# A planner's model of transfers, groups of first scores and due times of weights changed in a fused attention and two-MLP kernel

## The chip, the cores and the metric

One core of a Trainium2 chip runs the whole program. The metric is the device time of one execution in microseconds (us); lower is better. Instructions are spread by hand over five engines: PE (matrix products; PEld are its weight loads), DVE and ACT (elementwise work), POOL (unused here) and SP, which issues the DMA transfers.

## The reference, cut to what matters

Attention over two batches of 3008 tokens, without softmax, feeds two MLPs of 2048 hidden columns. All is float32.

```python
scores = (1.0 / S) * np.matmul(z, z.transpose(0, 2, 1))   # z: (2, 3008, 64)
attn = np.maximum(scores, 0.0) ** 2
x = (u * np.matmul(attn, v)).reshape(B * S, D)            # u, v: (2, 3008, 256)
h = x @ w_in;  x = (h - np.tanh(h)) @ w_out               # w_in: (256, 2048), w_out: (2048, 256)
h = x @ w2_in; return (np.maximum(h, 0) + alpha * np.minimum(h, 0)) @ w2_out
```

## The kernel before, in words

Every float32 operand is split into a high and a low part (a cast, here `high`, and a subtraction, here `low`), and PE multiplies high by high, high by low and low by high. So one score tile or one product needs elementwise work ahead of it, and it is that work which can be late.

The 6016 tokens form 12 blocks of up to 512 (six for each batch; the sixth has 448). For a block and a tile k of 128 keys, `score` puts z z^T into a PSUM bank. There are eight banks, and two of them collect the block's result. `relu` and `square` on ACT or DVE empty a score bank, `high` and `low` split the tile, and `back` multiplies it with v and adds to the block's two result banks. A score tile that belongs to two blocks is computed once. DVE transposes it (`transpose`), SP sends it to DRAM in four parts (`flip`), and it is read back for the other block (`load` of `l`). Scores are made in groups: `GROUPS` says how many tiles a group has, `LEADS` how many products ahead of its first use it stands on PE.

The MLPs' weights come as float64 words; `split_f64` makes high and low parts of them: one 512 KB load, six DVE instructions (L468 to L490) and one on ACT (L470) for each of 32 pieces. Pieces of the second MLP go back to DRAM (`spill`) until they are wanted. `W2_DUE` and `W1_DUE` spread the pieces' due times over a stretch of the attention part. From about 440 us on PE works on the MLPs (`front`, L658, and `back`, L726).

The order on every engine is set when the program is written: class `Plan` lists all operations, gives each a due time from PE's own order, and plays an event loop with assumed durations (`run`). Each engine takes, among the operations that are ready and have room, the one with the earliest due time; the order that results is what the chip executes, in that order on each engine. In this loop a transfer of 256 KB has `op.size` = 256 x 1.024 = 262, and the lines below add 262 / 290e3 = 0.0009 us for it to `pipe`: in effect every transfer is done 0.44 us (its issue) and 4.0 us (`LANDING`) after it is taken, whatever is in flight. `RESERVE`, `READY`, `FETCH`, `CAST_PENALTY`, `OTHER_PENALTY` and `TURNED` say how early an operation may take room or which engine it prefers. None of these numbers runs on the chip; they only decide the order.

On the chip, an instruction at the head of an engine's queue that waits holds up all that stand behind it, SP's transfers included.

```python
if e == SP:
    pipe = max(pipe, busy[e]) + op.size / 290e3
    op.done = pipe + (1.95 if t < 5.0 else LANDING)
```

## Time and profile before

| what | value |
|---|---|
| time, median of 3 runs (lowest to highest) | 1502.07 us (1500.44 to 1504.58) |
| profiled execution: own time | 1504.22 us |
| profiled execution: span from first to last instruction | 1502.4 us |
| PE busy | 1485.7 us, 99% of the span |
| PE weight loads busy | 1234.7 us, 82% |
| DVE busy | 1225.2 us, 82% |
| ACT busy | 1190.9 us, 79% |
| bytes moved by DMA | 133.59 MB |
| mean granted clock of PE | 0.996 |

PE is busy nearly all the time, so the span can be shortened, with the same products, only where PE stands idle or where its clock is granted at the lower of its two levels (1.2 instead of 2.4 GHz, shown as 0.5). The page's slices show that nearly all traffic of DMA lies in the first third of the span, where DVE is at its busiest too.

### The profile page before, as it was taken

To read this page: it belongs to the slowest core of one execution; us is meant where nothing else is said; L and a number is where in the kernel's file an instruction comes from. 1 tells how busy PE (TensorE), PEld (TensorE's weight loads), DVE (VectorE), ACT (ScalarE), POOL (GpSimd) and SP (SyncE) were. 2 spreads that over 40 slices of the span, in tenths; PEclk is the share of its full clock that TensorE was granted. 3 is DMA by queue.
4 is the path that set the end of the run, shared out by engine and by line. 5 is a ranking of instruction groups with operands and counts; after the bars stand their busy time and mean duration, and the time that the engine had idled before them with its cause. 6 is when DMAs were issued, how large, how long until landed. Compare 5 with 4: busy or idle time off the path is not lost.

```text
span 1502.4 us, 19557 instructions
## 1 busy us (share of the span) xinstructions
PE 1485.7 (99%) x6823; PEld 1234.7 (82%) x6823; DVE 1225.2 (82%) x2089; ACT 1190.9 (79%) x2282; POOL 0.2 (0%) x4
## 2 busy tenths in 40 slices
PE   8999999999999999999999999999999999999998
PEld 6777787777888888888888888888888888888888
DVE  8999978999989887777777877778777877778775
ACT  8777636887668888888888888888888888888853
POOL 0000000000000000000000000000000000000000
PEclk9999999999999999999999999999999999999999
DMA  5889884788862231100000000000000000000000
GB/s 186 236 274 296 274 285 139 231 267 249 259 208 83 76 117 50 49 1 1 29 1 27 1 29 1 10 19 1 27 1 28 1 28 1 1 27 1 15 1 27
DMA packets 116898, 133.59 MB, mean 89 GB/s; under 512 B 19904, under 2 KB 78912, under 8 KB 116800
## 3 DMA queue, kind: packets, MB, share of 16 engines
q1 hardware_dynamic: 116656, 132.24, 28.0%
q8 instruction: 53, 0.87, 0.2%
q14 instruction: 45, 0.37, 0.1%
q10 hardware_dynamic: 144, 0.11, 0.0%
HBM read 77.28 MB, written 50.86 MB: 85 GB/s over the span
## 4 chain that ended last, share of the span: by engine, by line
PE 89%; DVE 4%; DMA 3%; ACT 2%; issue 1%; SPq 1%; ACTq 0%; DVEq 0%
PE bank L726 52%; PE bank L658 34%; PE bank L569 3%; DMA mm<-flip 2%; DVE mm L393 1%; DMA raw<-in_v 1%; DVE flip L611 1%; DVE mm L638 1%; ACT raw L587 1%; ACT raw L595 1%; ACT mm L366 1%; DMA raw<-in_zT 0%; DVE mm L490 0%; DVE raw L474 0%; DVE raw L476 0%
## 5 line engine op out<-in xcount | busy, mean ns | idle before, releaser
L726 PE MATMUL bank<-mm,mm 128*128 128x512 f32 (+1 forms) x4008 | 966.0, 387 | 6.6 <-DVE mm L364 5.9
L726 PEld LDWEIGHTS bank<-mm,mm 128*128 128x128 f32 x4008 | 753.6, 189 | 156.1 <-DVE mm L364 6.8
L658 PE MATMUL bank<-mm,mm 128*128 128x512 f32 (+1 forms) x2304 | 575.7, 385 | 0.0
L658 PEld LDWEIGHTS bank<-mm,mm 128*128 128x128 f32 x2304 | 432.5, 188 | 80.8
L393 DVE TENSOR_TENSOR mm<-raw,mm 128x512 fp32r<-128x512 f32 (+1 forms) x586 | 389.7, 675 | 12.8 <-ACT mm L366 7.7
L676 ACT ACTIVATE raw<-raw 128x512 f32<-128x512 f32 (+1 forms) x576 | 360.0, 626 | 3.8
L676 ACT ACTIVATE raw<-bank 128x512 f32<-128x512 f32 (+1 forms) x384 | 207.0, 587 | 114.9 <-PE bank L658 114.5
L366 ACT CAST mm<-raw 128x512 fp32r<-128x512 f32 (+1 forms) x436 | 264.4, 624 | 20.5 <-DMA raw<-in_zT 8.9
L687 DVE TENSOR_TENSOR raw<-bank,raw 128x512 f32<-128x512 f32 (+1 forms) x192 | 130.4, 679 | 162.7 <-ACT raw L676 162.6
L695 ACT ACTIVATE raw<-bank 128x512 f32<-128x512 f32 (+1 forms) x384 | 218.2, 586 | 50.1 <-PE bank L658 44.7
L685 DVE TENSOR_TENSOR raw<-bank,raw 128x512 f32<-128x512 f32 (+1 forms) x192 | 130.2, 678 | 36.3 <-ACT raw L676 28.9
L697 DVE SCALAR_TENSOR_TENSOR raw<-raw,nalpha,raw 128x512 f32<-128x512 f32 (+1 forms) x192 | 140.6, 732 | 18.9 <-ACT raw L695 18.9
L689 DVE COPY_PREDICATED raw<-raw,raw 128x512 f32<-128x512 int32 (+1 forms) x192 | 142.5, 742 | 1.2
L587 ACT ACTIVATE raw<-bank 128x512 f32<-128x512 f32 (+1 forms) x146 | 74.6, 623 | 40.4 <-PE bank L569 40.2
L595 ACT ACTIVATE raw<-raw 128x512 f32<-128x512 f32 (+1 forms) x162 | 98.6, 677 | 0.0
L366 ACT CAST mm<-mm 128x512 fp32r<-128x512 f32 (+1 forms) x90 | 55.1, 623 | 45.5 <-DMA mm<-flip 45.3
L638 DVE TENSOR_TENSOR mm<-mm,mm 128x512 fp32r<-128x512 f32 (+1 forms) x120 | 78.7, 661 | 9.3 <-ACT mm L366 8.9
L611 DVE STREAM_TRANSPOSE flip<-raw 128x512 f32<-128x512 f32 x120 | 77.1, 684 | 2.9 <-DMA mm<-flip 2.4
L364 DVE CAST mm<-raw 128x512 fp32r<-128x512 f32 (+1 forms) x156 | 63.8, 415 | 9.6 <-ACT raw L595 4.9
L569 PE MATMUL bank<-mm,mm 64*128 64x512 f32 (+1 forms) x464 | 65.1, 406 | 3.8 <-DVE raw L589 3.7
L569 PEld LDWEIGHTS bank<-mm,mm 64*128 64x128 f32 x464 | 44.2, 187 | 19.1 <-issue 5.6
L470 ACT ACTIVATE raw<-raw 128x512 int32<-128x512 int32 x32 | 20.8, 651 | 25.9 <-DVE raw L468 25.8
(33 smaller groups left out, 245.0 us busy)
## 6 DMA issues: line engine op xcount, KB each, us to landing
flip<-flip SPq DMA_DIRECT2D x100, 256.0 KB, 4.3
mm<-flip SPq DMA_DIRECT2D x80, 256.0 KB, 4.8
mm<-flip SPq DMA_DIRECT2D x40, 224.0 KB, 4.2
st<-in_moe_w_in SPq DMA_DIRECT2D x16, 512.0 KB, 5.6
st<-in_moe_w_out SPq DMA_DIRECT2D x16, 512.0 KB, 5.0
raw<-in_v SPq DMA_DIRECT2D x24, 256.0 KB, 5.1
raw<-in_uT SPq DMA_DIRECT2D x20, 256.0 KB, 5.0
xd<-raw SPq DMA_DIRECT2D x20, 256.0 KB, 3.3
```

Source lines behind the costliest of these rows:

```text
L366: nc.scalar.copy(out=out, in_=in_)
L393: lambda e: nc.vector.tensor_sub(out=r32(l)[:, :n], in0=ap(), in1=f32(h)[:, :n]), [src, h], [l])
L569: nc.tensor.matmul(out=bank(keys[half])[:, :n], lhsT=key_weights(blocks[i][0], k, low, half), rhs=query_columns(x, half, n), start=j < 2, ...
L595: nc.scalar.activation(out=ap, in_=ap, func=AF.Square)
L658: nc.tensor.matmul(out=bank(ps)[:, :n], lhsT=r32(w)[:, o:o + P], rhs=r32(x)[:, :n], start=j == 0, stop=j == len(todo) - 1)
L676: add((name, out), {ACT: us}, lambda e: nc.scalar.activation(out=f32(out)[:, :n], in_=bank(inp)[:, :n] if inp is ps else f32(inp)[:, :n], ...
L685: add(("subtract", t), {DVE: dve_us(n)}, lambda e: nc.vector.tensor_sub(out=f32(t)[:, :n], in0=src(), in1=f32(t)[:, :n]), [ps], [t], limit ...
L687: add(("series", g), {DVE: dve_us(n)}, lambda e: nc.vector.tensor_mul(out=f32(g)[:, :n], in0=src(), in1=f32(g)[:, :n]), [ps], [g], limit=b ...
L689: add(("choose", t), {DVE: 0.05 + dve_us(n)}, lambda e: nc.vector.copy_predicated(out=f32(t)[:, :n], mask=f32(mask)[:, :n].bitcast(I32), d ...
L695: add(("relu2", out), {ACT: act_psum_us(n)}, lambda e, out=out, how=how: nc.scalar.activation(out=f32(out)[:, :n], in_=src(), func=AF.Relu ...
L697: add(("leak", r), {DVE: 0.06 + dve_us(n)}, lambda e: nc.vector.scalar_tensor_tensor(out=f32(r)[:, :n], in0=f32(q)[:, :n], scalar=nalpha_s ...
L726: nc.tensor.matmul(out=bank(accs[d])[:, :n], lhsT=r32(w)[:, c0:c0 + P], rhs=r32(x)[:, :n], start=first and e == 0, stop=last and e == len( ...
```

## The change

The planner's account of transfers changes: each transfer has a size in us of its own (0.7 by default for 256 KB, 2.3 for a float64 weight piece), starts no earlier than 1.9 us after its issue and behind the one before it, lands 3.0 us after its end, and no more than eight may be in flight. The first 24 score tiles come in groups of 4, 4, 8, 8 at fixed places (`FIRST`), batch 1's first block in 12, 12, and groups stand five products ahead instead of three. The due times of the weights move: the second MLP's from 70 to 270 us into 80 to 225 us, the first MLP's from 255 to 435 us into 290 to 437 us. The last block's second half is copied by DVE for SP's queue and by ACT for ACT's queue, where it was the other way round. What is computed, and how many products, stays as it was.

```diff
-GROUPS = ((8, 8, 8), (10, 10), (8, 8), (12,), (12,))
-LEADS = 3
-FIRST = 0
-RESERVE = ((15.0, 32), (5.0, 10), (1.5, 5), (0.0, 2))
-READY, FETCH = 20.0, 16.0
-CAST_PENALTY, OTHER_PENALTY = 4.0, 16.0
-TURNED = 22.0
-MARGIN, LANDING = 1.03, 4.0
-W2_DUE, W1_DUE = (70.0, 270.0), (255.0, 435.0)
+GROUPS = (((4, 4, 8, 8), (12, 12)), ((10, 10),) * 2, ((8, 8),) * 2, ((12,),) * 2, ((12,),) * 2)
+LEADS = 5
+FIRST = (0, 0, 1, 8)
+RESERVE = ((25.0, 30), (10.0, 14), (3.0, 6), (0.0, 2))
+READY, FETCH = 20.0, 22.0
+CAST_PENALTY, OTHER_PENALTY = 6.0, 10.0
+TURNED = 18.0
+MARGIN, LANDING, FIXED, FLYING = 1.03, 3.0, 1.9, 8
+W2_DUE, W1_DUE = (80.0, 225.0), (290.0, 437.0)
...
-            op.due = end - self.fastest(op) - op.tail - (3.0 if SP in op.engines else 0.0)
+            op.due = end - self.fastest(op) - op.tail - (op.size + FIXED + 2.0 if SP in op.engines else 0.0)
...
-                pipe = max(pipe, busy[e]) + op.size / 290e3
-                op.done = pipe + (1.95 if t < 5.0 else LANDING)
+                pipe = max(t + FIXED, pipe) + op.size
+                op.done = pipe + (0.1 if t < 5.0 else LANDING)
+                flying.append(op.done)
...
+                if e == SP:
+                    flying[:] = [at for at in flying if at > t + 1e-9]
+                    if len(flying) >= FLYING:
+                        continue
...
-            cuts = ((0, n), (0, n // 2, n))[d]
-            for e, (c0, c1) in enumerate(zip(cuts, cuts[1:])):
-                engine, queue = ((ACT, nc.sync), (DVE, nc.scalar))[e]
+            for e, (engine, c0, c1) in enumerate((((ACT, 0, n),), ((DVE, 0, n // 2), (ACT, n // 2, n)))[d]):
...
+                t = FIRST[g] if b == e == 0 else when[(0, *group[0])] - LEADS
+                bursts.setdefault(t, []).append(group)
```

What this does to the order is seen at three places. The first is ACT at the start of the program, behind its table load; `in_v` tiles are raw_142 and up before, and z tiles raw_145 and raw_146. Before:

```order
L366 CAST mm_68<-raw_142 128x512
L366 CAST mm_70<-raw_143 128x512
L366 CAST mm_71<-raw_144 128x512
L366 CAST mm_73<-raw_145 128x512
L366 CAST mm_75<-raw_146 128x512
L366 CAST mm_77<-raw_147 128x512
L587 ACTIVATE raw_155<-bank_171 128x512
```

In the change the same place reads as follows (raw_140, raw_143 and raw_144 are z, raw_142 and raw_145 are v):

```order
L372 CAST mm_67<-raw_140 128x512
L372 CAST mm_69<-raw_142 128x512
L372 CAST mm_71<-raw_143 128x512
L372 CAST mm_73<-raw_144 128x512
L593 ACTIVATE raw_153<-bank_171 128x512
L372 CAST mm_74<-raw_145 128x512
L601 ACTIVATE raw_153<-raw_153 128x512
L593 ACTIVATE raw_158<-bank_173 128x512
```

Six casts stood ahead of the first relu (L587); now there are four, one of them of a tile that is loaded second. Three v tiles come after it.

The second place is SP's queue where the z tiles of batch 1 are loaded (`in_zT`, `in_z_last`), shortly before that batch's first scores. Before (L494 and L484 are spills, which wait for DVE to finish a weight piece):

```order
L743 DMA raw_152<-in_uT 128x448
L513 DMA st_163<-in_moe_w_in 128x1024
L494 DMA w_wil_0_3_243<-mm_138 128x512
L408 DMA raw_156<-in_zT 128x512
L408 DMA raw_162<-in_zT 128x512
L408 DMA raw_161<-in_zT 128x512
L484 DMA w_wih_1_3_244<-raw_149 128x512
L428 DMA raw_154<-in_z_last 128x256
```

In the change (L641 reads a flipped tile back; the last spill of the second MLP's weights is now L500):

```order
L414 DMA raw_157<-in_zT 128x512
L490 DMA w_woh_7_250<-raw_144 128x512
L500 DMA w_wol_7_251<-mm_132 128x512
L749 DMA raw_156<-in_uT 128x448
L749 DMA raw_152<-in_uT 128x448
L641 DMA mm_86<-flip_4_5_204 128x448
L641 DMA mm_69<-flip_4_5_204 128x448
L641 DMA mm_83<-flip_4_5_204 128x448
L641 DMA mm_95<-flip_4_5_204 128x448
L414 DMA raw_146<-in_zT 128x512
L414 DMA raw_153<-in_zT 128x512
L434 DMA raw_141<-in_z_last 128x256
```

The third z tile moved ahead of the weights' spills, and no spill stands between the last loads any more; all spills of the second MLP's weights are now ahead of them.

The third place is DVE where it first takes a relu (L589, then L595) of batch 1. Before, steps of weight pieces (L468, L476, L488, L490) and v splits (L393) stand just ahead of it and between:

```order
L488 TENSOR_SCALAR raw_146<-raw_149 128x512
L393 TENSOR_TENSOR mm_123<-raw_160,mm_70 128x512
L468 TENSOR_SCALAR raw_145<-st_163 128x512
L490 SCALAR_TENSOR_TENSOR mm_98<-raw_158,raw_146 128x512
L393 TENSOR_TENSOR mm_77<-raw_151,mm_118 128x512
L393 TENSOR_TENSOR mm_131<-raw_141,mm_74 128x512
L476 SCALAR_TENSOR_TENSOR raw_145<-st_163,raw_145 128x512
L393 TENSOR_TENSOR mm_122<-raw_161,mm_115 128x512
L589 TENSOR_SCALAR raw_143<-bank_172 128x512
L468 TENSOR_SCALAR raw_142<-st_164 128x512
L589 TENSOR_SCALAR raw_144<-bank_171 128x512
```

In the change:

```order
L644 TENSOR_TENSOR mm_69<-mm_69,mm_106 128x448
L644 TENSOR_TENSOR mm_83<-mm_83,mm_123 128x448
L644 TENSOR_TENSOR mm_95<-mm_95,mm_74 128x448
L399 TENSOR_TENSOR mm_68<-raw_146,mm_105 128x512
L399 TENSOR_TENSOR mm_79<-raw_153,mm_129 128x512
L595 TENSOR_SCALAR raw_145<-bank_177 128x512
L595 TENSOR_SCALAR raw_143<-bank_172 128x512
L595 TENSOR_SCALAR raw_154<-bank_176 128x512
L595 TENSOR_SCALAR raw_162<-bank_170 128x512
L595 TENSOR_SCALAR raw_144<-bank_171 128x512
```

The weights' steps are gone from here; what is left ahead of the relus are splits of flipped tiles (L644) and of z (L399).

## Rows read from the trace of the kernel before

**Rows 1.** Windows of the whole span: busy us (instructions) by engine, granted clock, DMA:

```profile
core 0: us, PE busy (x) PEld busy (x) DVE busy (x) ACT busy (x) POOL busy (x), PEclk, DMA share, GB/s
...
8.19:12.43 4.24, 0.01 (x3) 0.00 (x1) 3.42 (x7) 4.12 (x9) 0.00 (x0) 1.00 1.05 399
12.43:15.88 3.45, 3.45 (x8) 2.65 (x9) 3.45 (x7) 3.45 (x8) 0.00 (x0) 0.51 0.66 251
15.88:237.94 222.06, 219.56 (x1075) 177.45 (x1074) 200.27 (x370) 149.13 (x288) 0.00 (x0) 1.00 0.81 254
237.94:241.65 3.71, 0.00 (x1) 0.00 (x1) 3.71 (x8) 3.67 (x9) 0.00 (x0) 0.93 0.21 79
241.65:247.99 6.34, 6.34 (x19) 5.08 (x20) 5.22 (x11) 5.70 (x13) 0.00 (x0) 0.50 0.11 41
...
1498.40:1502.40 4.00, 0.00 (x0) 0.00 (x0) 0.39 (x1) 0.34 (x1) 0.00 (x0) 0.79 0.32 115
sum 1502.40, PE 1485.73 PEld 1234.68 DVE 1225.16 ACT 1190.93 POOL 0.20; mean PE 185.72 PEld 154.33 DVE 153.14 ACT 148.87 POOL 0.03
```

**Rows 2.** Waits of PE, whole span: us in total, times, longest us:

```profile
PE bank L726 <- DVE mm L364: 5.9, 2, 4.2
PE bank L569 <- DVE raw L589: 4.5, 2, 3.7
...
PE bank L726 <- DVE mm L638: 0.7, 1, 0.7
```

**Rows 3.** Timeline of PE, 8 to 36 us: start, us, what (merged):

```profile
12.43 8.73 PE L726 MATMUL bank<-mm,mm 128*128 128x512 f32 x30 [4.23 <-DVE mm L364]
21.08 3.12 PE L569 MATMUL bank<-mm,mm 64*128 64x512 f32 x24
24.14 11.20 PE L726 MATMUL bank<-mm,mm 128*128 128x512 f32 x48
```

**Rows 4.** Timeline of ACT, 4 to 15 us:

```profile
6.50 3.91 ACT L366 CAST mm<-raw 128x512 fp32r<-128x512 f32 x6 [4.28 <-DMA raw<-in_v]
10.32 1.08 ACT L587 ACTIVATE raw<-bank 128x512 f32<-128x512 f32 x2
11.28 0.63 ACT L595 ACTIVATE raw<-raw 128x512 f32<-128x512 f32 x1
```

**Rows 5.** Timeline of DVE, 3 to 15 us:

```profile
7.15 3.98 DVE L393 TENSOR_TENSOR mm<-raw,mm 128x512 fp32r<-128x512 f32 x6 [1.47 <-ACT mm L366]
11.95 0.43 DVE L364 CAST mm<-raw 128x512 fp32r<-128x512 f32 x1 [0.81 <-ACT raw L595]
```

**Rows 6.** The chain that ended last, 224 to 243 us: start, us, what:

```profile
228.44 0.69 DVE mm L490
...
229.15 0.33 SPq L494
...
230.04 5.30 DMA raw<-in_zT
...
240.99 0.61 DVE raw L589
```

**Rows 7.** DMA issues at 215.07 and at 215.62 us: KB, us to landing:

```profile
st<-in_moe_w_in SPq DMA_DIRECT2D x1, 512.0 KB, 7.3
mm<-flip SPq DMA_DIRECT2D x1, 224.0 KB, 7.6
```

**Rows 8.** Waits of all engines, 100 to 118.5 us:

```profile
ACT mm L366 <- DMA mm<-flip: 5.4, 2, 4.8
DVE raw L476 <- ACT raw L470: 3.8, 1, 3.8
```

**Rows 9.** Timeline of all engines, 1497 to 1503 us:

```profile
1498.35 1.70 SPq L775 DMA_DIRECT2D outT<-raw  x2
1498.40 0.39 DVE L364 COPY raw<-bank 128x224 f32<-128x224 f32 x1 [4.45 <-PE bank L726]
...
1499.35 0.34 ACT L366 COPY raw<-bank 128x224 f32<-128x224 f32 x1 [1.02 <-DVE raw L364]
```

**Rows 10.** DMA issues of the whole span, results: KB, median us to landing:

```profile
outT<-raw SPq DMA_DIRECT2D x3, 224.0 KB, 1.9
```

**Rows 11.** Lines by form, 16 to 440 us: count, busy us, mean ns, idle before:

```profile
L476 DVE SCALAR_TENSOR_TENSOR raw<-st,raw 128x512 uint32<-128x512 uint32 x32 | 21.8, 681 | 5.3 <-ACT raw L470 5.3
...
L468 DVE TENSOR_SCALAR raw<-st 128x512 uint32<-128x512 uint32 x32 | 13.3, 416 | 1.6 <-DMA st<-in_moe_w_in 1.6
```

More of the change, by code (lines that the diff above doesn't have):

```diff
@@ L160, in run @@
         pipe = 0.0
+        flying = []
         left = len(self.ops)
@@ L366, in copy_on, with dma @@
             nc.scalar.copy(out=out, in_=in_)
-    def dma(name, emit, reads=(), writes=(), kb=256, limit=None, horizon=1e9, holds=()):
+    def dma(name, emit, reads=(), writes=(), us=0.7, limit=None, horizon=1e9, holds=()):
         return add(name, {SP: 0.44}, lambda e: emit(nc.sync), reads, writes, limit=limit, horizon=horizon,
-                   tail=0.0, size=kb * 1.024, holds=holds)
+                   tail=0.0, size=us, holds=holds)
     def cast_us(n):
@@ L427, in need_z @@
         st2, kl = ("ks", b, c), ("kk", b, c)
-        dma(("load", st2), lambda q: q.dma_start(out=f32(st2)[:, :m], in_=z_last[b]), [], [st2], kb=128, horizon=40.0)
+        dma(("load", st2), lambda q: q.dma_start(out=f32(st2)[:, :m], in_=z_last[b]), [], [st2], us=0.35, horizon=40.0)
         add(("high", kl), cast_us(m), lambda e: copy_on(e, r32(kl)[:, :m], f32(st2)[:, :m]), [st2], [kl])
@@ L465, in u32 @@
             return f32(key).bitcast(U32)
-        dma(("load", st), lambda q: load(q, f32(st).bitcast(U32)), [], [st], kb=512, horizon=30.0)
+        dma(("load", st), lambda q: load(q, f32(st).bitcast(U32)), [], [st], us=2.3, horizon=30.0)
         add(("fields", t1), {DVE: 0.345}, lambda e: nc.vector.tensor_scalar(
@@ L529, in need_x @@
         dma(("load", st), lambda q: q.dma_start(out=stage()[:, :, :n], in_=x_dram[i][:, :, :n]),
-            [("xd", i, d) for d in range(KD)], [st], kb=512, horizon=14.0)
+            [("xd", i, d) for d in range(KD)], [st], us=1.9, horizon=14.0)
         for d in range(KD):
@@ L573, in score_group @@
             us = 3 * pe_us(max(blocks[i][2] for i, _ in pair)) * 1.02
-            us += 0.215 * ((p == 0) + (p == len(pairs) - 1))
+            us += 0.215 * ((p == 0 and lead) + (p == len(pairs) - 1))
             ops.append(add(("score", pair[0]), {PE: us}, emit, set(reads), keys, tail=0.21))
@@ L625, in score_tile @@
                     out=to.rearrange("(f r) c -> r f c", r=Q)[:, :, c + e * nt * Q:c + (e + 1) * nt * Q],
-                    in_=f32(buf)[p0:p0 + Q].rearrange("p (f c) -> p f c", c=P)[:, :, :nt * Q]), made_t, [fd], holds=[buf])
+                    in_=f32(buf)[p0:p0 + Q].rearrange("p (f c) -> p f c", c=P)[:, :, :nt * Q]), made_t, [fd], us=1.0, holds=[buf])
     flips = {}
@@ L635, in need_flipped @@
         dma(("load", l), lambda s: s.dma_start(out=f32(l)[:, :n], in_=flips[b, kb, q][e * P:(e + 1) * P]), reads, [l],
-            horizon=FETCH)
+            us=0.8, horizon=FETCH)
         add(("high", h), cast_us(n), lambda e: copy_on(e, r32(h)[:, :n], f32(l)[:, :n]), [l], [h])
@@ L743, in evacuate @@
                 dma(("load", x), lambda q, x=x, d=d: q.dma_start(out=f32(x)[:, :n], in_=uT[d * P:(d + 1) * P, t0:t0 + n]),
-                    [], [x], horizon=25.0)
+                    [], [x], us=0.85, horizon=25.0)
                 def gate(e, x=x, acc=acc):
@@ L768, in evacuate, with out @@
                 continue
-            cuts = ((0, n), (0, n // 2, n))[d]
-            for e, (c0, c1) in enumerate(zip(cuts, cuts[1:])):
-                engine, queue = ((ACT, nc.sync), (DVE, nc.scalar))[e]
+            for e, (engine, c0, c1) in enumerate((((ACT, 0, n),), ((DVE, 0, n // 2), (ACT, n // 2, n)))[d]):
                 yk = y + (e,)
+                def out(queue, yk=yk, rows=rows, c0=c0, c1=c1):
+                    queue.dma_start(out=outT[rows, b * S + s + c0:b * S + s + c1], in_=f32(yk)[:, :c1 - c0])
                 add(("copy", yk), {engine: act_psum_us(c1 - c0)}, lambda e, yk=yk, acc=acc, c0=c0, c1=c1: copy_on(
                     e, f32(yk)[:, :c1 - c0], bank(acc)[:, c0:c1]), [acc], [yk])
-                dma(("out", yk), lambda q, yk=yk, rows=rows, c0=c0, c1=c1, queue=queue: queue.dma_start(
-                    out=outT[rows, b * S + s + c0:b * S + s + c1], in_=f32(yk)[:, :c1 - c0]),
-                    [yk], [("const", "out", i, d, e)])
+                if e:
+                    add(("out", yk), {ACT: 0.4}, lambda e, out=out: out(nc.scalar), [yk], [("const", "out", i, d, e)],
+                        tail=2.0)
+                else:
+                    dma(("out", yk), out, [yk], [("const", "out", i, d, e)])
     streams = [[(0, i, k) for i in range(NBLK) for k in tiles_of[i % QB]]]
@@ L793, in attention_two_mlps_kernel @@
     for b in range(B):
-        for e, sizes in enumerate(GROUPS):
+        for e, both in enumerate(GROUPS):
+            sizes = both[b]
             qs = [e] if e < len(GROUPS) - 1 else range(e, QB)
@@ L797, in attention_two_mlps_kernel @@
             assert sum(sizes) == len(todo)
-            for size in sizes:
+            for g, size in enumerate(sizes):
                 group, todo = todo[:size], todo[size:]
-                bursts.setdefault(max(0, when[(0, *group[0])] - LEADS), []).append(group)
+                t = FIRST[g] if b == e == 0 else when[(0, *group[0])] - LEADS
+                bursts.setdefault(t, []).append(group)
     def warm(e):
@@ L821, in build @@
                 for group in bursts.get(t, ()):
-                    score_group(group, LEADS)
+                    score_group(group, t > 0)
             if 0 <= t + LOOKAHEAD < len(steps) and steps[t + LOOKAHEAD][0]:
```

2 lines of the change are left out of this document (1 added, 1 removed).

## The prediction

> **What bounds the kernel now.** I read the windows first. In the sum over the span PE is busy 1485.73 of 1502.40 us [rows 1]. The change alters no product, so all there is to win is the 16.7 us in which PE stands idle, and what its clock loses. The windows place both. PE idles 4.24 us at the start (8.19 to 12.43), and the granted clock is then 0.51 for 3.45 us; it idles 3.71 us from 237.94 on, and the clock is then 0.50 for 6.34 us; it idles 4.00 us after the last product [rows 1]. At 0.5 PE does half the work, so these slow stretches cost 3.45 x 0.49 = 1.7 us and 6.34 / 2 = 3.2 us. The list of PE's waits names the releasers: DVE casts (L364), 5.9 us in two waits of 4.2 and so 1.7 us; DVE relus (L589), 4.5 us in two waits of 3.7 and 0.8 us; a DVE subtraction (L638), 0.7 us [rows 2]. So six numbers hold what can be won: 4.2 + 1.7 at the start, 1.7, 0.8, 3.7 + 3.2 and 0.7 in the attention part, and a part of the last 4.0.
>
> Why is DVE late? The chain of work that ended last shows it for the longest wait: a spill (L494) stands on SP until DVE has made its piece at 229.13, the z load behind it is issued at 230.04 and takes 5.30 us, and z casts, v splits and weight steps run in front of the relu at 240.99 that frees a bank [rows 6]. ACT and DVE were not short of time before that; they were waiting in order. The same is seen around 117 us: ACT stands 4.8 us at a cast for a flipped tile, and DVE 3.8 us for ACT's part of a weight piece that is queued behind this cast [rows 8]. In both cases a transfer landed later than the plan thought. The plan in effect gave each transfer 4.44 us from issue to landing; a 512 KB load took 7.3 us and the 224 KB one behind it 7.6 us [rows 7].
>
> **The start.** ACT does six casts in 3.91 us from 6.50, one for each load that lands (0.65 us), and only then the first relu at 10.32 and the square at 11.28 [rows 4]. DVE casts the tile at 11.95, and PE starts at 12.43 [rows 3, 5]. Now ACT's first cast is of a z tile that has landed before 6.50, and three casts stand between 6.50 and the relu: 6.50 + 3 x 0.65 = 8.45. A relu of 0.54 (1.08 / 2), a v cast of 0.65 and the square of 0.63 bring us to 10.3, DVE's cast of 0.43 to 10.7, PE to about 10.75. That is 1.7 us sooner. The list of instructions has DVE free for it: two splits and a relu, 0.66 each (3.98 / 6), lie between 7.15 and 9.8 [rows 5], and one v split after them.
>
> On PE the next score group now stands behind the first product, not behind the fifth. Products of six matmuls take 11.20 / 8 = 1.4 us and pairs of scores 3.12 / 4 = 0.78 us at the full clock [rows 3]. Product: 10.75 to 12.15. Three pairs: to 14.5. The fourth pair needs two banks that the first of these pairs' relus free, and ACT comes to them late: from 10.3 on it has four relus, three squares, a cast and then those two. A relu holds it for 0.48 ((11.28 - 10.32) / 2), and I give squares and casts 0.63 less the same overlap, 0.55 [rows 4]: 10.3 + 4 x 0.48 + 4 x 0.55 + 2 x 0.48 = 15.4, a wait of 0.9 us. The pair and four products follow: 15.4 + 0.8 + 5.6 = 21.8. Before, the same work ended at 24.14 [rows 3]: 2.3 us are won, the slow clock of before included. That counts on the clock staying up through an idle time of 10.75 - 8.19 = 2.6 us. It fell in waits of 4.2 and 3.7 us, and the longest wait otherwise, of 1.7, left it up [rows 1, 2]; 2.6 lies between, a little nearer to 1.7 than to 3.7, so I take no fall; the second wait, of 0.9, is below those that left it up. If it falls, 1.7 us of the gain go.
>
> A sooner PE has less room behind it. In DVE's order 33 long and 6 short instructions and one half tile lie between the low parts of tiles 2 and 14 of the first block (23, 4 and one before); at 0.60 us (0.68 less an overlap of 0.08) and 0.34 that is 22.2 us. Tile 2's high part is ACT's cast, done at 10.3 + 1.9 + 2.2 = 14.4, its low part at 15.1, so tile 14's at 37.3. On PE three products, four pairs and six products lie between 21.8 and the product of tile 14: 21.8 + 9 x 1.4 + 3.1 = 37.5, and the low part is wanted four matmuls (0.9 us) later. So there is 1.1 us of room, and I cost it at nothing. **Start: 2.3 us won**, between 0.6 (the clock falls) and 2.6.
>
> **The waits of the attention part.** The plan now has transfers stand behind each other, 0.7 us for 256 KB. The DMA queue at its fullest moved 399 GB/s, which is 262 KB in 0.66 us [rows 1]: the price is right, and slightly long. Loads are therefore planned later, and what depends on them is queued behind other work that is ready, not ahead of it. The order bears that out at the batch change: the spills of the second MLP's weights stand ahead of the last z loads on SP, DVE has only five splits of flipped and z tiles ahead of its relus, and no weight step. Five of block 5's products, not three, stand on PE behind these scores to cover what follows. The twelve rows of SP from the third z tile to the last z load are 12 x 0.66 = 8 us; the flipped tiles among them wait for slots of tiles of block 5 that PE has used up some 15 products ahead of these scores, which is 18 us (a product of 448 columns is 1.4 x 448 / 512 = 1.2). So 3.7 + 3.2 are won there, and 1.7, 0.8 and 0.7 at the others: 10.1 us. Against that stands that I can see the order only, not the landings: I keep back two small waits of the size of those seen, 0.8 and 0.7, which makes **8.6 us won** (bounds 10.1, and 3.2 if a wait long enough for the clock stays).
>
> **The weights** are the cost of it. A piece is three DVE instructions of 0.681 and three of 0.416 us [rows 11], 3.3 us. By their due times the second MLP's 16 pieces are now begun by 225 us, by the order 16 instead of 13 ahead of the low part of block 5's tile 17. Three pieces are 9.9 us in a stretch in which DVE is busy 200.27 of 222.06 us [rows 1]: 210.2, or 95%. It fits, since the 22 us idle there were waits for ACT and transfers [rows 8, 11], and later, where the first MLP's pieces now begin at 290, there is as much less to do. I cost it at nothing; the cover is that idle time, and once it is used up every further us of DVE is one of PE.
>
> **The end.** ACT's last copy begins 1.02 us after the engine is free, at 1499.35, behind an issue on its queue that waits for DVE [rows 9]. Now ACT copies its half at 1498.4 and issues it itself. But SP's order puts the half that DVE copies ahead of the 224 KB that have been ready since 1498.35: DVE is done at 1498.8 [rows 9], and with some 0.4 for an issue the 224 KB go out at 1499.2 and land 1.9 us later [rows 10], at 1501.1. Before, SP's last issue ended at 1500.05 (1498.35 + 1.70) [rows 9], so it began some 0.4 sooner, at 1499.65, and its half as long send landed by 1501.5. **0.2 us won**, between 0 and 0.4.
>
> **Sum.** 2.3 + 8.6 + 0.2 = 11.1 us. The profiled execution had a span of 1502.4 and a time of its own of 1504.22, 2.15 over the median of 1502.07 of three runs; I set the gain against that median: 1502.07 - 11.1 = 1491.0, and a span near 1491.3.
>
> **Rivals.** *The long wait stays (0.08).* ACT's relus of batch 1 stand behind casts of the last three z loads. If these land after PE has come to the scores, which they do when the wait on SP for slots is 18 - 8 = 10 us longer than I count, 3.7 + 3.2 come back: 1491.0 + 6.9 = 1497.9. Against it stand the spills, which are gone from between those loads.
>
> *Transfers don't land in turn (0.05).* The plan has each land behind the one before. In the trace they do: the smaller transfer, issued 0.55 us after the 512 KB one, landed 0.3 + 0.55 = 0.85 us after it [rows 7]. If they don't, an operand comes as late as before, and one long wait with a fall of the clock (6.9 us) is back: 1497.9. The Trainium skill's page "DMA: Bandwidth & Descriptors", section "Queues, rings and completion order", says that completion is not in order for an issuing engine, as a transfer is split over up to 16 rings; by that rule this rival holds. The trace at these two issues shows the contrary.
>
> *Only the start is won (0.11).* Every wait that goes could be replaced by another: the ones listed sum to 6.9 + 3.2 us, and the order is still one of guesses. Then 1502.07 - 2.3 - 0.2 = 1499.6.
>
> *DVE becomes the bound, and the kernel slower (0.06).* If DVE's waits between 16 and 238 us stay at 21.8 us while 9.9 us of work are added, and the 2.3 us by which PE is sooner are no longer there, PE waits 9.9 + 2.3 more; in waits of 3.7 us and over the clock falls, twice at least (6.4): 1491.0 + 12.2 + 6.4 = 1509.6. It decides from the point where DVE's idle time in that stretch stays above 222 - 2.6 - 210 = 9 us. For it speaks that DVE was the releaser of every wait of PE [rows 2].
>
> **How the numbers follow.** Forecast 0.70, rivals 0.08, 0.05, 0.11 and 0.06. The forecast's own range is 1488 (10.1, 2.6 and 0.4 won are 13.1 us: 1489.0, and 1 us under it for the spread of the runs) to 1494.5 (the clock falls at the start, two more waits of 0.8 to 1.7 us). Forecast and the two rivals at 1497.9 hold 0.83: the range is 1487.5 to 1498.5. A difference under 0.3% (4.5 us) can't be told from none in this kernel, whose runs lie 4.1 us apart. Faster than 1497.6: 0.70 and half of the 0.13 at 1497.9, 0.76; within 0.3%: the other half and 0.11, 0.18; slower 0.06.
>
> **What would show it.** PE's first product near 10.8 us instead of 12.43, the clock at 1.00 behind it, and the sixth product near 21.8. No wait of PE over 2 us between 20 and 440 us, and no clock of 0.5 there. On SP, no z load that waits for a spill. DVE over 93% busy from 16 to 235 us. The last copy of ACT right after the last product. I am wrong if PE waits for a DVE relu or cast again at the batch change, or waits in small pieces all along between 30 and 120 us, where DVE's margin is thinnest.

## The result, and the profile after

The changed kernel took **1488.15 us** (median of 4 runs, 1487.82 to 1488.85), the kernel before 1502.53 us beside it (4 runs, 1500.44 to 1504.58): a ratio of **0.9905, 95% interval 0.9888 to 0.9922**, 14.4 us less. The forecast was 1491.0, in a range of 1487.5 to 1498.5. The profiled execution took 1488.38 us with a span of 1486.6, against a span of 1502.4 in [rows 1].

PE's waits over the whole span, as in [rows 2] (us in total, times, longest us). This is the whole list; the second row is the warm-up's wait for DVE's first memset:

```profile
PE bank L732 <- DVE mm L370: 2.4, 1, 2.4
PE bank L817 <- DVE raw L820: 1.4, 1, 1.4
```

The relus' 4.5 us, the subtraction's 0.7 and the 1.7 of the second cast are gone; of the longest cast wait 2.4 of 4.2 us are left. The windows, cut where [rows 1] were cut:

```profile
core 0: us, PE busy (x) PEld busy (x) DVE busy (x) ACT busy (x) POOL busy (x), PEclk, DMA share, GB/s
...
8.19:12.43 4.24, 2.50 (x8) 1.33 (x10) 4.24 (x10) 4.24 (x9) 0.00 (x0) 0.85 1.06 399
12.43:15.88 3.45, 3.45 (x22) 2.75 (x24) 2.89 (x6) 2.61 (x6) 0.00 (x0) 0.69 0.54 185
15.88:237.94 222.06, 222.05 (x1098) 181.26 (x1095) 208.34 (x378) 167.07 (x325) 0.00 (x0) 1.00 0.84 261
237.94:241.65 3.71, 3.71 (x18) 3.09 (x17) 3.71 (x8) 3.71 (x8) 0.00 (x0) 1.00 0.33 127
...
1482.45:1486.60 4.15, 0.00 (x0) 0.00 (x0) 0.39 (x1) 0.35 (x1) 0.00 (x0) 0.90 0.31 111
sum 1486.60, PE 1478.58 PEld 1231.88 DVE 1235.74 ACT 1194.33 POOL 0.20; mean PE 184.82 PEld 153.99 DVE 154.47 ACT 149.29 POOL 0.02
```

From 15.88 us on PE counts as busy all the time, at the full clock. In the first two of these windows the clock is below 1: its records show 0.5 for 3.41 us from 11.19 on. PE's timeline (start, us, what, idle before it and its releaser) has the start, to be held against [rows 3]:

```profile
9.93 2.39 PE L732 MATMUL bank<-mm,mm 128*128 128x512 f32 x6 [2.36 <-DVE mm L370]
12.25 4.13 PE L575 MATMUL bank<-mm,mm 64*128 64x512 f32 x24
16.31 9.79 PE L732 MATMUL bank<-mm,mm 128*128 128x512 f32 x42
```

**Where the time came from.** The next table gives the start of some products on PE (block, tile), read from the PE instructions of the profiled executions, and how long the stretch up to each one took.

| up to | before, at | after, at | won in the stretch |
|---|---|---|---|
| sixth product (0, 5) | 24.14 | 21.86 | 2.3 |
| product (2, 23) | 125.42 | 120.49 | 2.6 |
| product (4, 0) | 177.76 | 171.12 | 1.7 |
| product (8, 23) | 359.12 | 343.50 | 9.0 |
| end of the last product | 1498.36 | 1482.42 | 0.3 |
| end of the span | 1502.4 | 1486.6 | -0.1 |

Together 15.8 us: 2.3 at the start, 13.6 in the attention part and behind it, nothing at the end. Against the medians it is 14.4, since the profiled execution of before was itself 2 us above its median.

### The profile page after: what moved, and what is told of

Read it like the earlier page. It is cut to its first block, busy times and chain, and to the rows that moved or that the text cites. A ratio compares the mean times of both kernels' runs of the same rounds, so it can differ in the third digit from the quotient of the medians.

```text
span 1486.6 us, 19633 instructions
## 1 busy us (share of the span) xinstructions
PE 1478.6 (99%) x6823; PEld 1231.9 (83%) x6823; DVE 1235.7 (83%) x2075; ACT 1194.3 (80%) x2296; POOL 0.2 (0%) x4
## 4 chain that ended last, share of the span: by engine, by line
PE 99%; DVE 0%; issue 0%; ACT 0%; ACTq 0%
PE bank L732 60%; PE bank L664 35%; PE bank L575 4%; PE bank L817 0%; DVE mm L399 0%; DVE raw L820 0%; DVE raw L370 0%; DVE mm L370 0%; ACT raw L372 0%; DVE raw L595 0%; ACTq L372 0%
## 5 line engine op out<-in xcount | busy, mean ns | idle before, releaser
L399 DVE TENSOR_TENSOR mm<-raw,mm 128x512 fp32r<-128x512 f32 (+1 forms) x586 | 385.6, 677 | 27.1 <-ACT mm L372 24.4
L682 ACT ACTIVATE raw<-bank 128x512 f32<-128x512 f32 (+1 forms) x384 | 206.9, 587 | 127.3 <-PE bank L664 125.5
L372 ACT CAST mm<-raw 128x512 fp32r<-128x512 f32 (+1 forms) x451 | 270.0, 625 | 11.3 <-DMA raw<-in_zT 5.3
L701 ACT ACTIVATE raw<-bank 128x512 f32<-128x512 f32 (+1 forms) x384 | 218.9, 587 | 42.1 <-PE bank L664 34.8
L593 ACT ACTIVATE raw<-bank 128x512 f32<-128x512 f32 (+1 forms) x127 | 65.7, 615 | 38.6 <-PE bank L575 37.9
L644 DVE TENSOR_TENSOR mm<-mm,mm 128x512 fp32r<-128x512 f32 (+1 forms) x120 | 78.0, 659 | 0.4 <-ACT mm L372 0.2
L372 ACT CAST mm<-mm 128x512 fp32r<-128x512 f32 (+1 forms) x107 | 63.4, 621 | 5.9 <-DMA mm<-flip 5.4
L476 ACT ACTIVATE raw<-raw 128x512 int32<-128x512 int32 x32 | 20.8, 649 | 52.6 <-DVE raw L474 52.5
L370 DVE CAST mm<-raw 128x512 fp32r<-128x512 f32 (+1 forms) x141 | 57.1, 414 | 6.8 <-DMA raw<-in_zT 2.1
```

Of the source, the lines that this page charges most:

```text
L372: nc.scalar.copy(out=out, in_=in_)
L399: lambda e: nc.vector.tensor_sub(out=r32(l)[:, :n], in0=ap(), in1=f32(h)[:, :n]), [src, h], [l])
L682: add((name, out), {ACT: us}, lambda e: nc.scalar.activation(out=f32(out)[:, :n], in_=bank(inp)[:, :n] if inp is ps else f32(inp)[:, :n], ...
L701: add(("relu2", out), {ACT: act_psum_us(n)}, lambda e, out=out, how=how: nc.scalar.activation(out=f32(out)[:, :n], in_=src(), func=AF.Relu ...
```

## The experiments

Two theories stood against each other at first. Theory 1: the account of transfers is what removes the waits of the attention part, since the plan now knows when an operand lands. The rival: other numbers of the change do it (groups, due times, rules), and the account is incidental. Below, "at the end of PE" is the end of PE's last product in the profiled execution: 1498.36 before, 1482.42 in the changed kernel, 1481.84 and 1482.45 in two more profiles of it (e5 and e12, nothing edited).

### e1: the account alone, on the kernel before

```diff
-                pipe = max(pipe, busy[e]) + op.size / 290e3
-                op.done = pipe + (1.95 if t < 5.0 else LANDING)
+                pipe = max(t + FIXED, pipe) + op.size
+                op.done = pipe + (0.1 if t < 5.0 else LANDING)
+                flying.append(op.done)
```

(with the sizes in us, the eight in flight, and the due times that belong to it; groups, rules, the weights' due times and last sends stay old)

> The kernel before with the new account of transfers alone (sizes, 1.9 us before a transfer starts, landing 3.0 us after its end, eight in flight); groups of scores, due times of weights and rules as before. Theory 1, the account takes the waits of the attention part away: the start stays as it was (a wait of some 4 us and the slow clock behind it), PE's waits from 20 to 440 us fall from 6.9 to under 2 us and no clock of 0.5 is left there, so the time is 1502.5 - 9 = 1493.5 us (1492 to 1496). Rival A, it is the groups and the five products of lead, and rival B, it is the weights' due times: waits of 5 us and more remain between 20 and 440 us, and the time is 1498 to 1503 us.

1491.37 us (1491.03 to 1492.59), where before took 1500.85 (8 runs) on the same chip: ratio 0.9939 [0.9924, 0.9953]. 9.5 us are won. PE's waits:

```profile
PE bank L732 <- DVE mm L370: 3.0, 2, 2.2
PE bank L811 <- DVE raw L814: 1.4, 1, 1.4
PE bank L732 <- DVE mm L399: 0.4, 1, 0.4
```

The two cast waits (2.2 and 0.9 us) lie at the start. The 3.7 us at the batch change, 1.7 at 117 us and 0.8 at 172 us are gone, a wait of 0.4 us at 282 us is new, and the clock did not fall. The account alone removes the long waits, those of before that theory 1 ascribed to it.

Two things theory 1 had not foreseen. The time is 0.6 us below its range. And the start did not stay as it was: the first product comes at 10.23 us and the sixth at 21.91, 2.2 us sooner than before and within 0.7 us of the changed kernel where that keeps the full clock too (21.18 in e5, 21.58 in e12), although the groups of four are not in it. In the profiles the last product ends 13.2 us sooner than before (at 1485.15), 11.0 of them behind the start. The edit brings the queueing, the eight in flight and the due times of transfers together; which of the three counts is not shown.

### e2: the changed kernel with the old account

```diff
-                pipe = max(t + FIXED, pipe) + op.size
-                op.done = pipe + (0.1 if t < 5.0 else LANDING)
-                flying.append(op.done)
+                pipe = max(pipe, busy[e])
+                op.done = pipe + (1.95 if t < 5.0 else 4.0)
```

(and the old due times of transfers, no limit on those in flight; all else as in the changed kernel)

> The changed kernel with the old account of transfers (in effect 4.44 us from issue to landing whatever is in flight), all else as changed. Theory 1: waits of 5 to 10 us come back between 20 and 440 us, among them one over 3 us with a slow clock behind it; 1493 to 1499 us. Rivals A and B: the waits stay away, under 2 us in sum, and the time is within 1.5 us of the change (1487 to 1490 us).

1495.35 us (1494.74 to 1497.41), ratio 0.9965 [0.9952, 0.9978]. PE's waits (the warm-up's left out):

```profile
PE bank L727 <- ACT mm L367: 3.6, 1, 3.6
PE bank L570 <- ACT raw L588: 2.2, 2, 1.9
...
PE bank L570 <- DVE raw L590: 0.8, 2, 0.5
```

The wait of 1.95 us ends at 169.47 us, and the clock is at 0.5 for 3.41 us from 169.77 on. The timelines of ACT and DVE ahead of it show the same thing as [rows 8]:

```profile
160.88 1.24 ACT L367 CAST mm<-mm 128x512 fp32r<-128x512 f32 x2 [2.76 <-DMA mm<-flip]
162.03 0.62 ACT L471 ACTIVATE raw<-raw 128x512 int32<-128x512 int32 x1
162.69 0.69 DVE L477 SCALAR_TENSOR_TENSOR raw<-st,raw 128x512 uint32<-128x512 uint32 x1 [1.90 <-ACT raw L471]
...
168.30 0.63 ACT L471 ACTIVATE raw<-raw 128x512 int32<-128x512 int32 x1 [1.77 <-DVE raw L469]
168.84 0.58 ACT L588 ACTIVATE raw<-bank 128x512 f32<-128x512 f32 x1
```

ACT stands 2.76 us at casts of two flipped tiles, which land 7.2 and 6.9 us after their issue, where this plan counts 4.44. A weight step (L471) is queued behind them, and DVE waits 1.90 us for it (L477). From there DVE is busy without a gap to 169.4 us, so its step of the next piece (L469, at 167.85) comes late, and ACT's step behind that too. Behind it stands the relu (L588) that frees a bank.

So late transfers cost time again, as theory 1 has it, and the time lies in its range. The waits are smaller than it said, 3.0 us in sum and 1.95 at most, not 5 to 10 with one over 3. Of the 8.9 us by which the last product ends later than in the changed kernel (1491.30), they are 3.0; the start costs 1.8 (sixth product at 23.64), the low clock at 169.77 us 1.9, and short waits inside groups of scores, to which e9 comes back, 2.3. The long wait at the batch change did not come back: without the account, the rest of the change keeps it away. The account alone wins 9.5 us, all the rest alone 5.5 (1500.85 - 1495.35); both together win 12.6 (e5) to 14.4, so 0.6 to 2.4 us are covered twice.

### e3: the changed kernel with the old groups, e4: with the old due times

```diff
-GROUPS = (((4, 4, 8, 8), (12, 12)), ((10, 10),) * 2, ((8, 8),) * 2, ((12,),) * 2, ((12,),) * 2)
-LEADS = 5
+GROUPS = (((8, 8, 8),) * 2, ((10, 10),) * 2, ((8, 8),) * 2, ((12,),) * 2, ((12,),) * 2)
+LEADS = 3
```

> The changed kernel with the old groups of scores and three products of lead, the new account and due times kept. Theory 1: only the start is lost, the first product begins at 11 to 12.5 us and the time is 1488 + 2.5 = 1490.5 us (1489.5 to 1492.5), with under 2 us of waits after 20 us. Rival A: the waits between 20 and 440 us come back, 1495 us and more.

```diff
-W2_DUE, W1_DUE = (80.0, 225.0), (290.0, 437.0)
+W2_DUE, W1_DUE = (70.0, 270.0), (255.0, 435.0)
```

> The changed kernel with the weights' old due times (70 to 270 and 255 to 435 us), all else as changed. Theory 1: the due times matter little, under 2 us of waits after 20 us, 1487 to 1490 us. Rival B: weight pieces stand among batch 1's first casts and relus again, a wait of over 3 us with the slow clock is back near 235 us, 1493 to 1497 us.

e3 took 1490.23 us (1490.0 to 1491.16), ratio 0.9929 [0.9913, 0.9946]. Its loss lies at the start; PE's timeline:

```profile
11.65 8.95 PE L732 MATMUL bank<-mm,mm 128*128 128x512 f32 x30 [3.46 <-DVE mm L370]
20.53 3.12 PE L575 MATMUL bank<-mm,mm 64*128 64x512 f32 x24
```

The sixth product starts at 23.57 us, 1.7 later than in the changed kernel, whose clock fell at the start as well: with the rest of the change in place, the old groups cost that much. e1, whose clock did not fall, has the sixth product at 21.91 us with the old groups too, so most of the start's gain does not need the new ones. At (2, 23) the kernel is 1.9 us later (122.36), at the end of PE 2.8 (1485.18). e4 took 1489.64 us (1488.66 to 1489.96), ratio 0.9925 [0.9910, 0.9939], with no wait behind the start; PE ends at 1483.51, 1.1 us later than in the changed kernel's profile, which has the same fall of the clock. The due times are worth about 1 us, too little to tell by these intervals from none.

### e5 to e8: control, old rules, the order of the last sends, the first relu

> The changed kernel once more, nothing edited, so that the other kernels can be set beside it on one chip. Theory 1 (the account of transfers did nearly all of it): ratio to before 0.990 to 0.992, 1486 to 1489 us, in its profile no wait of TensorE longer than 0.3 us between the first product of the outputs and the last. Rival (the first comparison was chance, as before itself spreads over some 4 us): ratio 0.993 or more.

e5: 1488.18 us (1487.69 to 1488.62); before took 1500.76 (9 runs) on this chip; ratio 0.9913 [0.9900, 0.9927]. PE waits 2.1 us at the start and never again.

```diff
-RESERVE = ((25.0, 30), (10.0, 14), (3.0, 6), (0.0, 2))
-READY, FETCH = 20.0, 22.0
-CAST_PENALTY, OTHER_PENALTY = 6.0, 10.0
-TURNED = 18.0
+RESERVE = ((15.0, 32), (5.0, 10), (1.5, 5), (0.0, 2))
+READY, FETCH = 20.0, 16.0
+CAST_PENALTY, OTHER_PENALTY = 4.0, 16.0
+TURNED = 22.0
```

> The changed kernel with the old planner numbers (the reserve of operand slots, READY, FETCH, the two penalties, TURNED), but the new account, the new groups, the new due times and the new last sends. Theory 1: these numbers only shift work that is early either way; within 2 us of the changed kernel, 1486.5 to 1490. Rival (the account alone would leave operands late and the smaller FETCH and reserve bring waits back): 1491 to 1495, with waits of 0.5 us or more between 100 and 250 us.

e6: 1491.19 us (1490.2 to 1491.74), 3.0 more than e5 and outside what theory 1 allowed by 1.2. Yet the list of waits has only one row more, of 0.3 us at 14.6 us. The loss is inside what the profile counts as busy. The sum of the windows from 0 to 1485 us, of e5:

```profile
sum 1485.00, PE 1478.15 PEld 1230.77 DVE 1236.09 ACT 1194.44 POOL 0.20; mean PE 1478.15 PEld 1230.77 DVE 1236.09 ACT 1194.44 POOL 0.20
```

and of e6:

```profile
sum 1485.00, PE 1480.66 PEld 1231.45 DVE 1222.94 ACT 1193.11 POOL 0.20; mean PE 1480.66 PEld 1231.45 DVE 1222.94 ACT 1193.11 POOL 0.20
```

PE is "busy" 2.5 us longer with the same products, at the same clock, and ends 2.5 us later (1484.36 against 1481.84). Compared group by group, all of it is lost in eight groups of scores between 64 and 389 us, 0.17 to 0.69 us each: small waits for banks, too short to be told from a matmul's end. The rival's range holds the time, but only one group (0.69 us at 161 us) lost as much as its 0.5 us. PE's own list leaves these waits out; the waits of its weight loads (PEld) for ACT's relus do show them. From 22 us on, in e5 and in e6:

```profile
PEld bank L575 <- ACT raw L593: 2.5, 11, 0.4
PEld bank L575 <- ACT raw L593: 4.9, 17, 0.5
```

e9 and e10 settle which of the rules they come from.

```diff
-                    dma(("out", yk), out, [yk], [("const", "out", i, d, e)])
+                    dma(("out", yk), out, [yk] + [("const", "out", i, 0, 0)] * d, [("const", "out", i, d, e)])
```

> The changed kernel with the last two transfers on SP's queue the other way round, so that the 224 KB block that is copied first also goes out first. Theory 1 (the last landing is set by the order on SP: the block copied first waits behind the half that is copied last): the last landing comes some 2.7 us after TensorE's last product, where it was 3.2 us; 0.3 to 0.7 us faster than the changed kernel on the same chip. Rival (the last landing is set by the copies and by the transfer's own time, whichever goes first): no difference over 0.2 us, the last landing 3.1 us or more after the last product.

e7: 1487.88 us (1487.28 to 1488.09), a median 0.3 below e5, with runs that overlap. The profile tells more than the times. The end in the changed kernel, timeline of all engines:

```profile
1481.85 0.53 ACT L372 COPY raw<-bank 128x448 f32<-128x448 f32 x1 [5.71 <-PE bank L732]
1482.45 0.39 DVE L370 COPY raw<-bank 128x224 f32<-128x224 f32 x1 [4.44 <-PE bank L732]
1482.91 0.81 SPq L779 DMA_DIRECT2D outT<-raw  x2
1482.93 0.35 ACT L372 COPY raw<-bank 128x224 f32<-128x224 f32 x1 [0.55 <-DVE raw L370]
1483.31 0.39 ACTq L779 DMA_DIRECT2D outT<-raw  x1
```

and in e7:

```profile
1481.89 0.53 ACT L372 COPY raw<-bank 128x448 f32<-128x448 f32 x1 [5.71 <-PE bank L732]
1482.45 0.81 SPq L779 DMA_DIRECT2D outT<-raw  x2
1482.49 0.39 DVE L370 COPY raw<-bank 128x224 f32<-128x224 f32 x1 [4.37 <-PE bank L732]
```

SP issues at 1482.45 instead of 1482.91, and the span ends 3.6 us behind PE's last product (1486.1 - 1482.46) where it was 4.2 (1486.6 - 1482.42). e11 below, which has the same edit, also ends 3.6 us behind it. So in the profiles the order on SP was worth the 0.5 us expected; the times alone, with runs that overlap, do not show it.

```diff
+    first = {("relu", ("a", 0, 0)): 4.45, ("high", ("vh", 0, 0)): 4.46, ("relu", ("a", 0, 1)): 4.46,
+             ("square", ("a", 0, 0)): 4.47, ("low", ("vl", 0, 0)): 4.47, ("high", ("h", 0, 0, 0)): 4.48,
+             ("low", ("l", 0, 0, 0)): 4.49}
+    for op in plan.ops:
+        op.start = first.get(op.name, op.start)
```

> The changed kernel with seven operations at the start set ahead by hand: on ScalarE the first tile's relu goes ahead of the cast of v and its square ahead of two casts of z, on VectorE the second tile's relu and the first tile's splits go ahead of the two z splits that only the third group needs. Theory 1 (TensorE's idle time before the first product of the outputs comes from the order on ScalarE, where the first relu stands behind three casts and the first of these waits for v's load; and the lower clock from 11.2 us on comes from that idle time): first product at 8 to 8.5 us where it was 9.93, no stretch at clock 0.5 in the start, 1.5 to 3.5 us faster than the changed kernel. Rival (the two engines are full, so that what is won at the first product is given back at the third group of scores, which waits for banks): first product at 8 to 8.5 us, but back 0,0,5 still at about 21.9 us, and within 0.5 us of the changed kernel.

e8: 1487.33 us (1486.8 to 1487.65), 0.85 below e5. PE's timeline:

```profile
8.05 1.63 PE L732 MATMUL bank<-mm,mm 128*128 128x512 f32 x6 [0.15 <-DVE mm L370]
...
13.59 1.46 PE L575 MATMUL bank<-mm,mm 64*128 64x512 f32 x6 [0.74 <-ACT raw L593]
```

The first product comes at 8.05 us, 2.3 us sooner than in e5 (10.35), so the wait did come from ACT's order. But the third group of scores waits for banks, and the sixth product starts at 20.55 against 21.18: 0.6 of the 2.3 us are kept. The gain of 0.85 us lies between the two expectations (1.5 to 3.5, and under 0.5), and both had half of it: the wait is one of order, and what it hid is that ACT and DVE have no more to give. From 8 to 14 us ACT is busy for 6.00 and DVE for 5.97 of 6.00 us.

### e9 to e12: which rule, both improvements, control

```diff
-CAST_PENALTY, OTHER_PENALTY = 6.0, 10.0
+CAST_PENALTY, OTHER_PENALTY = 4.0, 16.0
```

> The changed kernel with the two old penalties alone (CAST_PENALTY 4, OTHER_PENALTY 16), which say how unwilling the plan is to give DVE work that ACT could do. The kernel with all the old planner numbers had lost 2.5 us by the last product, in waits of 0.1 to 0.6 us of score pairs for banks. Theory A (the penalties did it: relus stay on ACT, and banks come free late): 1489.5 to 1491.5, TensorE's last product 1.5 to 2.5 us later than in the changed kernel, in the same small waits at score pairs. Theory B (the reserve, FETCH and TURNED did it, by which tiles hold slots or transfers come late): within 0.7 us of the changed kernel run beside it.

```diff
-RESERVE = ((25.0, 30), (10.0, 14), (3.0, 6), (0.0, 2))
-READY, FETCH = 20.0, 22.0
-TURNED = 18.0
+RESERVE = ((15.0, 32), (5.0, 10), (1.5, 5), (0.0, 2))
+READY, FETCH = 20.0, 16.0
+TURNED = 22.0
```

> The changed kernel with the old RESERVE, FETCH and TURNED and the new penalties, the other part of the kernel with all the old planner numbers. Theory A: within 0.7 us of the changed kernel. Theory B: 1489.5 to 1491.5, with its loss in waits of 0.1 to 0.6 us between 60 and 400 us.

e11 puts e7's and e8's edits together and sets one more operation pair back, the second v tile's split:

```diff
-             ("low", ("l", 0, 0, 0)): 4.49}
+             ("low", ("l", 0, 0, 0)): 4.49, ("high", ("vh", 0, 1)): 9.45, ("low", ("vl", 0, 1)): 9.83}
```

> The changed kernel with the first relu and square set ahead, with the second v tile's split set behind the first relus as well, and with the 224 KB block first in the last sends. If the gains of the two edits add (0.65 us by the last product, 0.55 us behind it), and the wait of 0.7 us in the third group of scores goes with the cast of v that stood ahead of its relus: 1486 to 1487, 1.2 to 2.0 us below the changed kernel on the same chip. If the two engines are full in the first 16 us, the third group waits as before and 1.2 us at most are won.

> The changed kernel with nothing edited, beside the other three on one chip: 1487.5 to 1489.

Before took 1501.39 us (9 runs) on this chip, e12, the control, 1488.41 (1487.55 to 1488.96). e9 took 1490.58 (1490.17 to 1491.65), 2.2 more; e10 1488.62 (1488.56 to 1489.39), 0.2 more. Theory A holds: from the sixth product to the end of PE, e9's profile is 2.5 us longer than e12's, as much as e6's is longer than e5's. (Its last product ends 3.2 us later, more than the 1.5 to 2.5 expected; 0.7 of them come from the start, where e9's clock fell.) Theory B falls by its times, but e10 is not free either: its profile is 0.9 us longer there, made up in part by a sixth product 0.5 us sooner.

One of the places is shown by the timelines of PE, ACT and DVE and, from 22 us on, the weight loads' waits of e9

```profile
164.81 2.54 PE L575 MATMUL bank<-mm,mm 64*128 64x512 f32 x16
163.38 3.97 ACT L593 ACTIVATE raw<-bank 128x512 f32<-128x512 f32 x8 [2.59 <-PE bank L575]
165.48 1.46 DVE L595 TENSOR_SCALAR raw<-bank 128x512 f32<-128x512 f32 x2 [0.98 <-PE bank L575]
PEld bank L575 <- ACT raw L593: 4.8, 18, 0.5
```

and of e12:

```profile
163.64 1.84 PE L575 MATMUL bank<-mm,mm 64*128 64x512 f32 x16
162.23 1.30 ACT L593 ACTIVATE raw<-bank 128x512 f32<-128x512 f32 x2 [1.98 <-PE bank L575]
162.20 2.09 DVE L595 TENSOR_SCALAR raw<-bank 128x512 f32<-128x512 f32 x3 [1.58 <-PE bank L575]
PEld bank L575 <- ACT raw L593: 2.3, 11, 0.2
```

The same 16 matmuls take 0.70 us more, at a granted clock of 1.00 in both, and PE's own waits have no row for it. In e12 ACT and DVE begin this group's relus together, and the fourth is done 2.40 us behind the group's first matmul (161.19). In e9 ACT takes the first five one behind the other while DVE stands idle for 0.98 us, and the fourth is done 3.07 us behind the first matmul (162.37). So it is as theory A says: relus stay on ACT, and banks come free late. Over the whole attention part DVE takes 24 of the 168 relus in e9, 33 in e10, 41 in e12.

e11 took 1487.16 us (1487.03 to 1487.97), 1.25 below e12, and is with e8 the fastest seen; ratio to before 0.9904 [0.9890, 0.9918]. The gain lies on the border of the two expectations (1.2). By the wait the second one holds: in the third group it did not go, it grew, and ACT and DVE are busy for all of the 6 us from 8 to 14 us. PE's timeline of e11:

```profile
7.89 1.66 PE L732 MATMUL bank<-mm,mm 128*128 128x512 f32 x6 [0.15 <-DVE mm L370]
9.48 2.62 PE L575 MATMUL bank<-mm,mm 64*128 64x512 f32 x18
13.43 1.45 PE L575 MATMUL bank<-mm,mm 64*128 64x512 f32 x6 [1.33 <-ACT raw L593]
14.81 11.45 PE L732 MATMUL bank<-mm,mm 128*128 128x512 f32 x42
```

and of e12:

```profile
10.81 1.93 PE L732 MATMUL bank<-mm,mm 128*128 128x512 f32 x6 [2.40 <-DVE mm L370]
12.67 3.42 PE L575 MATMUL bank<-mm,mm 64*128 64x512 f32 x24
16.03 9.80 PE L732 MATMUL bank<-mm,mm 128*128 128x512 f32 x42
```

In e11's profiled execution the clock then fell as well (0.5 for 3.41 us from 15.08 on): the 42 matmuls take 11.45 us instead of 9.80, 1.65 us given back. Its other three runs took 1487.03 to 1487.25 us at a mean granted clock of 1.000, which such a fall would lower to 0.999 (3.41 x 0.5 / 1486 = 0.001).

## Why the prediction was right, step by step

**The attention part: right in mechanism, too small by 5 us.** The step took 8.6 us; 13.6 were won there. Two things were mis-sized. I kept back 1.5 us for new small waits, and there were none in the list of waits. And "six numbers hold what can be won" was wrong: I took PE's idle time and the slow clock for all there was. PE's busy time fell from 1485.73 [rows 1] to 1478.58 us with the same products. The clock explains 3.2 of these 7.1 us (1.7 + 3.2 of before, less 3.41 / 2 = 1.7 after); 3.9 us were waits inside "busy", 3.5 of them behind the sixth product (8.6 + 1.5 + 3.5 = 13.6). The prediction has no term for them: I read the order for its long waits alone.

e6 and e9 show what a part of them is: short waits of score pairs for banks. To compare the kernels, take the time from each matmul of scores to the next beyond the 0.23 us that a pair takes where nothing waits, from the sixth product on and outside the low clock. The kernel before spends 2.2 us more in this way than the changed kernel, e1 0.8, e2 2.3, e6 2.5, e9 2.6. So both the account and the penalties govern these waits, and neither alone: e1 has the old penalties, e2 the new ones. The other 1.3 us lie mostly between the matmuls of products and were not traced.

**The batch change: right.** No z load stands behind a spill that waits for DVE any more. The last two tiles, issued at 214.46 and 215.07 us, landed some 4.9 us later, 6.6 us ahead of the batch's first scores on PE (226.51); in the kernel before the last tile landed at 235.97, 0.4 us behind the first scores (235.57). Who waits there is turned round. The waits of the other engines from 16 to 250 us, in the changed kernel:

```profile
ACT raw L593 <- PE bank L575: 20.9, 8, 6.5
DVE raw L595 <- PE bank L575: 9.5, 6, 6.1
```

Relus now wait for PE's scores, up to 6.5 us, where PE waited 3.7 us for a relu [rows 2]. e1 shows that the account alone removes this wait, e2 that the rest of the change removes it too; the prediction did not tell the two apart.

**The start: the sum was right by luck, the parts were not.** 2.3 us won, as forecast, and the sixth product at 21.86 where I had 21.8. But the first product came at 9.93 and not at 10.75, 0.8 us sooner; the clock fell, which I had taken as not happening and which costs 1.7 us; and the wait of 0.9 us for banks did not come, as PE was slow enough for ACT, which waits 0.73 us for PE there. The three make up for each other: 0.8 + 0.9 - 1.7 = 0. In the two control profiles the clock did not fall, and the first product came at 10.35 and 10.81, the sixth at 21.18 and 21.58. So "if it falls, 1.7 us of the gain go" did not hold either: the sixth product is 0.3 to 0.7 us sooner without the fall. Why the first product moves about is seen in the landings of the first loads: the third z tile, which the casts ahead of the first relu need, landed at 6.37 us in the profile after, at 6.79 in e5 and at 7.25 in e12, in the same place of the same queue. In e12 the first relu starts at 8.45 us and the first product at 10.81, as reckoned (8.45 and 10.75), and the fourth pair at 14.88, where I had 15.4: of the 0.9 us wait there some 0.3 is left. PE's own waits have no row for it; its weight loads wait 0.4 and 0.3 us for ACT there.

**The weights: the sum was right, its parts were not.** DVE is busy 208.34 of 222.06 us from 15.88 on, 93.8% (forecast 210.2, over 93%), and PE's list has no wait from it. But of the 8.1 us that DVE gained there, weight steps are 6.2 (two pieces more in that window, 16 for 14, not three), relus 4.9 (18 for 11) and splits of z and v and the gates 5.8, while 20 casts fewer (14 for 34) take 8.2 us off; ACT has 24 casts more. The penalties' part in this is not in the prediction. With the old due times (e4) DVE is as busy there, 210.12 us, so it is not the weights' due times that fill it. e4 puts these at some 1 us.

**The end: wrong in sign, at a size that no time shows.** 0.2 us won was forecast, 0.1 to 0.2 were lost: the last landing comes 3.20 us behind PE's last product (3.02 before), the span's end 4.19 (4.08). What failed is the 1.9 us from issue to landing. SP issues the 224 KB last, 0.92 us behind the last product, near the 0.84 that I had; but it lands 2.28 us later, and the half-size transfer of before took 1.67. "Now ACT copies its half at 1498.4" failed too: ACT begins 0.55 us after it could, behind DVE's copy of the other half. Both halves lie in one bank, and the program has ACT wait for DVE. The Trainium skill's page "PSUM — Partial Sum Buffer", section "PSUM bank collisions raise a hardware error", says that two engines must not access one bank and quadrant at once, also if both only read, and that the compiler adds a dependence between them; the trace agrees (0.55 us of waiting <-DVE raw L370). So here the two copies ran one behind the other, although on two engines.

**The rivals.** Transfers did land in turn: of the 475 on SP's queue, not one landed ahead of the one issued before it, in the trace of before and in that of after. The Trainium skill's page "DMA: Bandwidth & Descriptors", section "Queues, rings and completion order", says that completion is not in order for an issuing engine; no transfer here shows it. The long wait did not stay, and more than the start was won. DVE did not become the bound, but the point that I gave for it was wrong: its idle time stayed at 13.7 us (222.06 - 208.34), above the 9 us from which I had PE lose. From 16 to 250 us 9.5 us of its idle time is relus that wait for PE, which is room, not a loss.

## What to carry to other kernels

A plan that issues transfers by estimated landings should count what is already in flight; here such an account was worth 9.5 us by itself, since each operand that lands later than planned holds up everything behind it on its engine. What can be won is not PE's idle time alone: compare PE's busy time with that of another order of the same products before saying what is left, and read the waits of its weight loads, which have rows where PE's own list has none. And before an operation is moved ahead, ask what the engines do behind it: 2.3 us won at the first product were 0.6 us a few products later.
